# Pairs of score tiles, a new step order, and 8 KB rows for weight loads in a fused attention and soft-MoE kernel

## The chip, the cores and the metric

One core of a Trainium2 chip. TensorE (PE) does the matmuls, VectorE (DVE), ScalarE (ACT) and GpSimd (POOL) the rest; SyncE (SP) issues the DMAs from its queue, in order, and 16 DMA engines carry them. The metric is the device time of one execution in microseconds, as the median of several runs. The profiles come from the hardware profiler and hold one execution each.

## What is computed

```python
# 8 batches x 8 heads x 576 tokens x 64; attention only inside chunks of 64 tokens
scores = q_c @ k_c.T / 8
attn = softmax(scores)
x = (attn @ v_c)            # -> 4608 tokens x 512

logits = x @ phi            # 512 x 32: 8 experts x 4 slots
d = softmax(logits, over the 4608 tokens)
slot_input = d.T @ x        # 32 x 512
for e in range(8):
    slot_out[e] = relu(slot_input[e] @ w1[e]) @ w2[e]   # 512 x 1024, 1024 x 512
x = softmax(logits, over the 32 slots) @ slot_out

h = x @ w_in                # 4608 x 1024, 64-bit words on the host's side
u = h * softmax(h)
out = layernorm(u) * g_ln @ w_out
```

`moe2_w_in` and `moe2_w_out` reach the chip as 64-bit words, which the kernel itself turns into fp32.

## The kernel before, in words

The 4608 tokens are 36 tiles of 128. The program has three parts, and every engine's order is written out by hand, so an engine that waits holds up all that stands behind it on that engine.

**The loop over tiles** (L517, steps i = 0 to 33). A step works on several tiles at once: the scores `S` of tile i (`pe_S`, L251: per pair of heads two matmuls on column halves of PE), their maximum `mx`, the subtraction `sub` (L268) and `exp`; the transpose `PT` of tile i-1 and its copy `PTe`; the product with v, `x` (L295), of tile i-2 with its row sums `rz`, `rc` and the multiply `xm`; the transpose `xT` of tile i-3 and its copy `xTe`; every fourth step the logits `LT` and the running softmax over tokens (`lte`, `L`, `mT`, `z`, `sl`, `acc`). Beside it, from step 2, one of 32 chunks c of 64-bit words is converted on ACT, DVE and POOL (`sq`, `t`, `u`, `m`, `a`, `add`, `mul`). The order of the operations in a step is one of the four lines of `STEP` (L29), taken by i mod 4; an operation that a step doesn't have is skipped. The scores go to `sx`, one PSUM tile of two banks, bank i mod 2 (L249).

**Loads.** All are issued from SP, at the place of their name in the step: `qk` loads the keys and queries of tile i+4 into one of four buffers as two DMAs of 64 rows of 4 KB, on the even and on the odd partitions; `v` loads two tiles of v in every second step; `raw` (L185) loads the words of two chunks, 512 KB, into one of three buffers; `W` (L492) loads expert weights. These are 64 loads of 512 KB, m = 0 to 63, 4 KB on each of 128 partitions. `PACE` (L35) says how many are to be issued by each step. A load takes the next free place: first the 23 of the ring, and after the loop the buffers that the loop no longer needs, handed over by `own_c`, `own_q`, `own_v`, `own_p`, `own_t` and `own_x` (L787). `used_w` (L135) gives places back, two at a time, once the matmuls of two loads are issued; what is loaded there waits on SP for them. Before the loop `FIRST` (L44) issues the first loads.

**The expert tail** runs in the order of the list `ORDER` (L45): the last tiles, the slot inputs (`si`), then the experts' first layer `w1_...` (L932), the second layer `w2_...` (L968) and the last 16 loads' matmuls `wc48` to `wc63` (L982), which use the loads in the order of m. Between them stand transposes and copies for the next part. `x34` (L580) puts the product of tile 34 into `sx`.

**The loop over output tiles** (L1393 and around it) takes the second MLP for 36 tiles: 24 matmuls `o_ps` and two `h_ps` a tile, with the copies, the exponentials and two DMA transposes.

The lines of the step order before, and the weights' matmuls for one pair of loads:

```python
FIRST = "cs qk0 qk1 qk2 v0 raw0 qk3 g phi v2 raw2 raw4"
        for k in range(2):
            for j in range(4):
                nc.tensor.matmul(
                    h[32 * j:32 * j + 4, :], siT[:, 2 * kp + k, 4 * G + j, :], wt[m0 + 2 * k + j // 2][j % 2], ...
                )
            used_w(m0 + 2 * k, m0 + 2 * k + 1)
```

Of the kernel before, what the change touches and what calls it, by code (L numbers as in the profile page):

```python
# [9 lines left out]
F32 = mybir.dt.float32  # L10
# [3 lines left out]
U32 = mybir.dt.uint32  # L14
# [7 lines left out]
RING = 23  # L22
NRAW = 32
# [6 lines left out]
S a m t x xT u mT qk rz PT mx v xTe sub PTe W rc add mul raw exp xm mn d sq de  # L30
S a x u raw v m qk rz sl mx t W rc z xT sub xTe PT PTe add xm acc mul sq exp
m t S u a x qk rz xT mx W sub xTe PT rc acc v PTe add LT xm mul sq raw exp lte
t m a S x u raw L tm v mx xT add qk PT lall rz mul xTe sub rc PTe W sq xm exp
# [10 lines left out]
FIRST = "cs qk0 qk1 qk2 v0 raw0 qk3 g phi v2 raw2 raw4"  # L44
# [23 lines left out]
def soft_moe_kernel(ctx: ExitStack, tc, qkT, v1, w12, w64, phi, g_ln, cst, out):  # L68
# [49 lines left out]
    def w_tile(p):  # L118
        return lambda: [p.tile([128, 2, 512], F32, tag="w", name="w")]

    def load_w(n):
        while n > 0 and free and wloads:
            n -= 1
            m = wloads.pop(0)
            place[m] = free.pop(0)
            t = place[m]()
            if len(t) == 1:
                gated("w", nc.sync.dma_start(out=t[0], in_=w12[m]))
                wt[m] = [t[0][:, k, :] for k in range(2)]
            else:  # L130
                for k in range(2):
                    nc.sync.dma_start(out=t[k], in_=w12[m, :, k])
                wt[m] = t

    def used_w(*ms):  # L135
        for m in ms:
            if place[m] not in gone:
                free.append(place[m])
        load_w(len(free))

    gone = []
    free.extend([w_tile(ring)] * RING)
# [42 lines left out]
    def load_raw(c):  # L185
        if c < NRAW and c % 2 == 0:
            raw = cvp.tile([128, 2, 256, 2], U32, tag="raw", name="raw", bufs=3)
            raw_t[c], raw_t[c + 1] = raw[:, 0], raw[:, 1]
            gated("raw", nc.sync.dma_start(out=raw.rearrange("p k n t -> p (k n t)"), in_=w64[c // 2].bitcast(U32)))
# [45 lines left out]
    def cv_c(c):  # L235
# [4 lines left out]
        **{f"raw{i}": lambda i=i: load_raw(i) for i in range(6)},  # L240
# [8 lines left out]
    sx = ps1.tile([128, 2, 512], F32, name="s_ps")  # L249

    def pe_S(i):  # L251
        s = sx[:, i % 2, :]
# [218 lines left out]
    def step_ops(i):  # L471
# [9 lines left out]

        def rc():
# [9 lines left out]
        def W():  # L492
            load_w(pace[i + 1] - pace[i])
# [6 lines left out]
            S=(True, lambda: pe_S(i)), qk=(True, lambda: load_qk(i + 4)),  # L500
# [997 lines left out]
```

## Time and profile before

| | us |
|---|---|
| median of 3 runs | 403.44 (402.84 to 403.8) |
| the profiled execution | 402.77 |
| its span, first to last instruction | 401.0 |
| PE busy | 382.4 (95%) |
| DVE busy | 311.0 (78%) |
| ACT busy | 224.3 (56%) |
| POOL busy | 200.2 (50%) |
| granted TensorE clock, mean | 1.000 of full |

The busy time of PE counts matmuls whose ends are modelled, and they overlap: a PE that is 95% busy need not be at its peak. PEld is PE's weight load, which shows the pace of the matmuls better. The DMA share is the mean busy time of the 16 engines; it can be a little over 1, since packets of one engine overlap. All times in the profile are counted from the first instruction. A row of the timeline is one or several like instructions: its start, the time they took together, engine and line, operands and count, and in brackets how long the engine had been idle and for whom it waited.

### The profile page before, as it was taken

To read this page: it belongs to the slowest core of one execution; us is meant where nothing else is said; L and a number is where in the kernel's file an instruction comes from. 1 tells how busy PE (TensorE), PEld (TensorE's weight loads), DVE (VectorE), ACT (ScalarE), POOL (GpSimd) and SP (SyncE) were. 2 spreads that over 40 slices of the span, in tenths; PEclk is the share of its full clock that TensorE was granted. 3 is DMA by queue.
4 is the path that set the end of the run, shared out by engine and by line. 5 is a ranking of instruction groups with operands and counts; after the bars stand their busy time and mean duration, and the time that the engine had idled before them with its cause. 6 is when DMAs were issued, how large, how long until landed. Compare 5 with 4: busy or idle time off the path is not lost. (4 is left out here: it accounts for less than half of the span.)

```text
span 401.0 us, 10317 instructions
## 1 busy us (share of the span) xinstructions
PE 382.4 (95%) x3947; PEld 220.4 (55%) x3947; DVE 311.0 (78%) x777; ACT 224.3 (56%) x470; POOL 200.2 (50%) x201
## 2 busy tenths in 40 slices
PE   3799899999999999999999999999999999999997
PEld 2577777777787642354544444444444444444445
DVE  3788788989886449574989799999888888888840
ACT  1577877877785512332577765556554555455521
POOL 2577767777778246330123255555455544454430
PEclk9999999999999999999999999999999999999999
DMA  7999999999999999991156757777665666557671
GB/s 231 403 409 408 389 397 397 409 407 407 410 397 408 401 396 406 409 391 26 30 103 146 140 134 159 159 158 148 144 140 135 144 151 133 132 137 158 132 159 52
DMA packets 101153, 99.20 MB, mean 247 GB/s; under 512 B 78064, under 2 KB 78704, under 8 KB 101104
## 3 DMA queue, kind: packets, MB, share of 16 engines
q1 hardware_dynamic: 101104, 98.54, 77.1%
q8 instruction: 31, 0.51, 0.5%
q14 instruction: 18, 0.15, 0.1%
HBM read 70.60 MB, written 9.44 MB: 200 GB/s over the span
## 5 line engine op out<-in xcount | busy, mean ns | idle before, releaser
L1194 POOL TENSOR_SCALAR uh<-u,sc 128x1024 f16<-128x1024 f32 (+1 forms) x35 | 65.1, 1860 | 51.1 <-issue 38.3
L1393 PEld LDWEIGHTS <-uhT 128*128 128x128 f16 x560 | 52.1, 98 | 68.3 <-issue 8.8
L1393 PE MATMUL o_ps<-xb,uhT 128*128 128x512 f16 x280 | 66.7, 380 | 0.7 <-DMA uhT<-uh 0.7
L1393 PE MATMUL o_ps<-xb,ulT 128*128 128x512 f16 x280 | 66.3, 379 | 0.0
L1393 PE MATMUL o_ps<-wo,uhT 128*128 128x512 f16 x280 | 66.1, 379 | 0.0
L1322 ACT ACTIVATE e<-h_ps,nm 128x1024 f32<-128x1024 f32 x34 | 37.8, 1113 | 43.7 <-DVE nm L1316 43.7
L1210 ACT ACTIVATE e<-u,nmean 128x1024 f32<-128x1024 f32 x35 | 40.1, 1147 | 28.7 <-DVE nmean L1209 28.7
L256 PE MATMUL s_ps<-qk 128*64 128x128 f32 x576 | 41.1, 287 | 9.3 <-DMA qk<-in_qkT 6.5
L1360 POOL TENSOR_TENSOR a<-a,mhalf 128x1 f32<-128x1 f32 x36 | 21.8, 606 | 56.2 <-DVE a L1377 42.5
L1316 DVE TENSOR_REDUCE nm<-h_ps 128x1 f32<-128x1024 f32 x34 | 41.5, 1220 | 9.3 <-PE h_ps L1311 9.3
L1185 DVE SCALAR_TENSOR_TENSOR u<-h_ps,e 128x1024 f32<-128x1024 f32 x35 | 42.8, 1223 | 6.1 <-ACT e L1322 6.1
L1393 PEld LDWEIGHTS <-ulT 128*128 128x128 f16 x280 | 27.3, 98 | 33.1 <-issue 0.3
L1370 DVE SCALAR_TENSOR_TENSOR ul<-u,sc,uh 128x1024 f16<-128x1024 f32 x35 | 45.3, 1295 | 0.0
L256 PEld LDWEIGHTS s_ps<-qk 128*64 128x64 f32 x576 | 32.5, 141 | 16.2 <-issue 10.3
L398 ACT ACTIVATE xt_b<-xt_ps 128x512 f32<-128x512 f32 (+1 forms) x37 | 21.6, 586 | 17.8 <-PE xt_ps L416 16.9
L265 DVE TENSOR_REDUCE mx<-s_ps 128x8 f32<-128x512 f32 x36 | 24.6, 684 | 8.5 <-PE s_ps L256 8.0
L1411 ACT ACTIVATE ob<-o_ps,a 128x512 f32<-128x512 f32 x35 | 23.8, 679 | 9.3 <-PE o_ps L1393 8.0
L219 POOL TENSOR_SCALAR conv<-conv 128x256 f32<-128x256 f32 x16 | 17.6, 1099 | 21.8 <-ACT conv L206 21.8
L1311 PE MATMUL h_ps<-s,c4T 128*128 128x512 f32 x68 | 27.4, 485 | 0.0
L277 ACT ACTIVATE p<-p 128x512 f32<-128x512 f32 x35 | 21.7, 621 | 6.6 <-DVE p L271 6.6
L271 DVE TENSOR_TENSOR p<-s_ps,mx 128x512 f32<-128x512 f32 x35 | 24.1, 690 | 0.9
L229 POOL TENSOR_TENSOR conv<-conv 128x256 int32<-128x256 int32 x32 | 23.3, 729 | 2.6
(232 smaller groups left out, 633.5 us busy)
## 6 DMA issues: line engine op xcount, KB each, us to landing
w<-in_w SPq DMA_DIRECT2D x45, 512.0 KB, 8.0
qk<-in_qkT SPq DMA_DIRECT2D x72, 256.0 KB, 6.8
vall<-in_v SPq DMA_DIRECT2D x18, 520.0 KB, 6.7
out<-ob SPq DMA_DIRECT2D x35, 256.0 KB, 2.1
raw<-in_w SPq DMA_DIRECT2D x16, 512.0 KB, 6.4
qk<-in_w SPq DMA_DIRECT2D x4, 512.0 KB, 9.0
w_raw<-in_w SPq DMA_DIRECT2D x3, 512.0 KB, 9.0
vall<-in_w SPq DMA_DIRECT2D x3, 512.0 KB, 8.9
```

The costliest lines, as they stand in the source:

```text
L256: nc.tensor.matmul(s[ts(c, 64), ts(g, 128)], b[:, 1, ts(2 * g + c, 64)], b[:, 0:3:2, ts(2 * g + c, 64)], start=True, stop=True, tile_posit ...
L265: mark("mx", nc.vector.tensor_reduce(out=mx, in_=s, axis=AX.X, op=ALU.max))
L271: mark("sub", nc.vector.tensor_tensor(out=p, in0=s, in1=mx.unsqueeze(2).to_broadcast([128, 8, 64]), op=ALU.subtract,))
L1185: nc.vector.scalar_tensor_tensor(out=u, in0=d["h"], scalar=1.0, in1=e, op0=ALU.mult, op1=ALU.mult, accum_out=zz[:, 1:2])
L1194: nc.gpsimd.tensor_scalar(out=uh[:, 0:n], in0=u[:, 0:n], scalar1=d["sc"][:, 1:2], scalar2=1.0, op0=ALU.mult, op1=ALU.mult)
L1210: nc.scalar.activation(out=d["e"], in_=d["u"], func=AF.Square, bias=nmean, scale=1.0, accum_out=d["zz"][:, 2:3])
L1311: nc.tensor.matmul(h[:, ts(n, 512)], c4T[:, i, :], s4[n], start=True, stop=True)
L1316: nc.vector.tensor_reduce(out=nm, in_=st[i]["h"], axis=AX.X, op=ALU.max, negate=True)
L1322: nc.scalar.activation(out=d["e"], in_=d["h"], func=AF.Exp, bias=d["nm"], scale=1.0, accum_out=d["zz"][:, 0:1])
L1370: nc.vector.scalar_tensor_tensor(out=ul, in0=d["u"], scalar=d["sc"][:, 1:2], in1=d["uh"], op0=ALU.mult, op1=ALU.subtract)
L1393: nc.tensor.matmul(d["o"], lt(n % 8), w(n % 8), start=(n == 0), stop=(n == 23))
L1411: nc.scalar.activation(out=ob, in_=d["o"], func=AF.Copy, scale=d["a"][:, 7:8])
```

## The change

Six things are changed together.

- `S` of a step with even i computes the scores of tiles i and i+1; odd steps have none. The two banks are two tiles (`s_banks`) in a pool of their own, which is closed in `x34`, where `sx` is made.
- The four lines of `STEP` are new.
- `FIRST` ends with `phi qk3`; `v2` and `raw2` are issued behind the `qk` load of step 0, and `raw4` behind that of step 1 (`THEN`).
- Expert weights are stored in pairs, 8 KB a partition. The ring is 11 places of two loads (22 in place of 23). A pair is loaded by `halves`: one DMA of 64 rows of 8 KB for the even partitions, one for the odd. Where only a place of one load is free, a load goes there in rows of 4 KB as before. Some of the loop's buffers are handed over as places of two (`raw0`, `raw1`, `v0`, `xt`), and they can be used again.
- The 64-bit words are stored and loaded four chunks at a time, 1 MB, into one of two buffers, also by `halves`; the first eight chunks come as four loads of two chunks in rows of 4 KB as before.
- `W` counts by the places that are free, so that the ring is filled to `PACE`.

```diff
@@ -19,7 +19,7 @@
...
-RING = 23
+RING = 11
...
@@ -27,10 +27,10 @@
...
-S a m t x xT u mT qk rz PT mx v xTe sub PTe W rc add mul raw exp xm mn d sq de
-S a x u raw v m qk rz sl mx t W rc z xT sub xTe PT PTe add xm acc mul sq exp
-m t S u a x qk rz xT mx W sub xTe PT rc acc v PTe add LT xm mul sq raw exp lte
-t m a S x u raw L tm v mx xT add qk PT lall rz mul xTe sub rc PTe W sq xm exp
+S x t v m a rz xT u qk xTe PT mT PTe mx W sub add rc exp mul xm mn sq d raw de
+S mx xT qk x PT a u sub z m W raw add PTe rz sl exp t rc mul xm v acc xTe sq
+S m mx t x u W a acc xT rz PT xTe raw add LT mul sub rc PTe v sq exp lte qk xm
+x u S qk a m v t add rz mx sub xT L raw PT tm PTe rc xTe mul xm lall sq exp W
...
@@ -41,7 +41,8 @@
...
-FIRST = "cs qk0 qk1 qk2 v0 raw0 qk3 g phi v2 raw2 raw4"
+FIRST = "cs qk0 qk1 qk2 v0 raw0 g phi qk3"
+THEN = {0: 'v2 raw2', 1: 'raw4'}
...
@@ -115,31 +116,55 @@
...
-    def w_tile(p):
-        return lambda: [p.tile([128, 2, 512], F32, tag="w", name="w")]
+    def halves(out, in_):
+        for a in range(2):
+            nc.sync.dma_start(out=out[a:128:2], in_=in_[a:128:2])
+    def ring_place():
+        return ring.tile([128, 4, 512], F32, tag="w", name="w")
...
     def load_w(n):
...
-            n -= 1
-            m = wloads.pop(0)
-            place[m] = free.pop(0)
-            t = place[m]()
-            if len(t) == 1:
-                gated("w", nc.sync.dma_start(out=t[0], in_=w12[m]))
-                wt[m] = [t[0][:, k, :] for k in range(2)]
+            m = wloads[0]
+            wide = [f for f in free if f[0] == 2]
+            one = [f for f in free if f[0] == 1]
+            if m % 2 == 0 and wide and free[0][0] == 2:
+                if n < 2:
+                    return
+                f = wide[0]
+            elif one:
+                f = one[0]
...
-                for k in range(2):
-                    nc.sync.dma_start(out=t[k], in_=w12[m, :, k])
-                wt[m] = t
+                return
+            free.remove(f)
+            n -= f[0]
+            t = f[1]()
+            for k in range(f[0]):
+                place[wloads.pop(0)] = f
+            if f[0] == 2:
+                halves(t, w12[m // 2])
+                for k in range(4):
+                    wt.setdefault(m + k // 2, []).append(t[:, k, :])
+            else:
+                src = w12[m // 2, :, ts(m % 2, 2), :]
+                if len(t) == 1:
+                    nc.sync.dma_start(out=t[0], in_=src)
+                    wt[m] = [t[0][:, k, :] for k in range(2)]
+                else:
+                    for k in range(2):
+                        nc.sync.dma_start(out=t[k], in_=src[:, k])
+                    wt[m] = t
+    def places():
+        return sum(f[0] for f in free)
...
     def used_w(*ms):
-        for m in ms:
-            if place[m] not in gone:
-                free.append(place[m])
-        load_w(len(free))
-    gone = []
-    free.extend([w_tile(ring)] * RING)
+        f = place[ms[0]]
+        if f[0] == 2:
+            free.append(f)
+        load_w(places())
+    free.extend((2, ring_place) for _ in range(RING))
...
@@ -183,10 +208,16 @@
...
     def load_raw(c):
-        if c < NRAW and c % 2 == 0:
-            raw = cvp.tile([128, 2, 256, 2], U32, tag="raw", name="raw", bufs=3)
-            raw_t[c], raw_t[c + 1] = raw[:, 0], raw[:, 1]
-            gated("raw", nc.sync.dma_start(out=raw.rearrange("p k n t -> p (k n t)"), in_=w64[c // 2].bitcast(U32)))
+        if c < NRAW and c % 4 == 0:
+            raw = cvp.tile([128, 4, 256, 2], U32, tag="raw", name="raw", bufs=2)
+            for k in range(4):
+                raw_t[c + k] = raw[:, k]
+            raw_t["q", c // 4] = raw.rearrange("p k n t -> p (k n t)")
+            if c >= 8:
+                halves(raw_t["q", c // 4], w64[c // 4].bitcast(U32))
+        if c < 8 and c % 2 == 0:
+            b = slice(512 * (c % 4), 512 * (c % 4) + 1024)
+            nc.sync.dma_start(out=raw_t["q", c // 4][:, b], in_=w64[c // 4].bitcast(U32)[:, b])
...
@@ -246,10 +277,13 @@
...
-    sx = ps1.tile([128, 2, 512], F32, name="s_ps")
+    pss = ctx.enter_context(ExitStack())
+    ps_s = pool("ps_s", 1, pss, space=PSUM)
+    s_banks = [ps_s.tile([128, 512], F32, name="s_ps", tag=f"s{a}") for a in range(2)]
+    sx = None
...
     def pe_S(i):
-        s = sx[:, i % 2, :]
+        s = s_banks[i % 2]
...
@@ -479,6 +513,11 @@
...
+        def q():
+            load_qk(i + 4)
+            for o in THEN.get(i, "").split():
+                first_loads[o]()
         def rc():
...
@@ -490,14 +529,14 @@
...
         def W():
-            load_w(pace[i + 1] - pace[i])
+            load_w(pace[i + 1] - 22 + places())
...
         return dict(
...
-            S=(True, lambda: pe_S(i)), qk=(True, lambda: load_qk(i + 4)),
+            S=(i % 2 == 0, lambda: (pe_S(i), pe_S(i + 1))), qk=(True, q),
...
@@ -578,6 +617,9 @@
...
     def x34():
+        nonlocal sx
+        pss.close()
+        sx = pool("ps_sx", 1, pss, space=PSUM).tile([128, 2, 512], F32, name="s_ps")
...
@@ -761,8 +803,8 @@
...
     def raw_home():
-        raw = cvp.tile([128, 2, 256, 2], U32, tag="raw", name="w_raw", bufs=3)
-        return [raw.rearrange("p k n t -> p k (n t)").bitcast(F32)]
+        raw = cvp.tile([128, 4, 256, 2], U32, tag="raw", name="w_raw", bufs=2)
+        return raw.rearrange("p k n t -> p k (n t)").bitcast(F32)
...
     def p_pair():
...
@@ -772,12 +814,12 @@
...
     homes = dict(
-        raw0=raw_home, raw1=lambda: raw_home(), raw2=lambda: raw_home(),
+        raw0=(2, raw_home), raw1=(2, raw_home),
...
-        v=lambda: [va[:, 0:1024].rearrange("p (a b) -> p a b", a=2)],
-        **{f"v{i}": lambda i=i: [va[:, ts(i, 1024)].rearrange("p (a b) -> p a b", a=2)] for i in (1, 2)},
+        v0=(2, lambda: va[:, 0:2048].rearrange("p (a b) -> p a b", a=4)),
+        v2=lambda: [va[:, ts(2, 1024)].rearrange("p (a b) -> p a b", a=2)],
...
-        xt0=lambda: [XT[:, 0:2].rearrange("p t g n -> p t (g n)")], xt1=lambda: [XT[:, 2:4].rearrange("p t g n -> p t (g n)")],
+        xt=(2, lambda: XT.rearrange("p t g n -> p t (g n)")),
...
@@ -786,17 +828,15 @@
...
     def own(*names):
...
-            free.append(homes[k])
-            if k[0] not in "vp":
-                gone.append(homes[k])
-        load_w(len(free))
-    op("loadw")(lambda: load_w(len(free)))
-    op("own_c", "S34 x32 loadw")(lambda: own("qk0", "qk1", "qk2", "qkx", "raw0", "raw1", "raw2", "conv"))
+            free.append(homes[k] if isinstance(homes[k], tuple) else (1, homes[k]))
+        load_w(places())
+    op("loadw")(lambda: load_w(places()))
+    op("own_c", "S34 x32 loadw")(lambda: own("qk0", "qk1", "qk2", "qkx", "raw0", "raw1", "conv"))
...
-    op("own_v", "x34 x351 own_q")(lambda: own("v", "v1", "v2", "pt"))
+    op("own_v", "x34 x351 own_q")(lambda: own("v2", "v0", "pt"))
...
-    op("own_t", "own_p LT35")(lambda: own("xt0", "xt1"))
+    op("own_t", "own_p LT35")(lambda: own("xt"))
...
@@ -1475,10 +1516,10 @@
     arrays = {
...
-        "w12": np.stack(w12),
+        "w12": np.stack(w12).reshape(32, 2, 128, 2, 512).transpose(0, 2, 1, 3, 4).reshape(32, 128, 4, 512),
...
-            bits64(inputs["moe2_w_in"]).reshape(4, 128, 2, 512).transpose(0, 2, 1, 3).reshape(8, 128, 512),
-            bits64(inputs["moe2_w_out"]).reshape(8, 128, 512),
+            bits64(inputs["moe2_w_in"]).reshape(4, 128, 1024),
+            bits64(inputs["moe2_w_out"]).reshape(4, 2, 128, 512).transpose(0, 2, 1, 3).reshape(4, 128, 1024),
...
```

## Rows read from the trace of the kernel before

**Rows 1.** The page: span, and DMA share in 40 slices, in tenths

```profile
span 401.0 us, 10317 instructions
...
DMA  7999999999999999991156757777665666557671
```

**Rows 2.** The chain of waits that ended last: start us, us, what

```profile
206.86 5.35 PE o_ps L1393 x24
```

**Rows 3.** Windows: us, busy us of PE, PEld, DVE, ACT, POOL, clock, DMA, GB/s

```profile
20.00:120.00 100.00, 96.68 (x1932) 76.46 (x1927) 86.46 (x215) 76.80 (x202) 75.47 (x88) 1.00 1.02 403
145.00:183.50 38.50, 37.35 (x457) 15.63 (x460) 27.52 (x53) 9.51 (x17) 18.09 (x16) 1.00 0.99 376
```

**Rows 4.** Timeline of all engines, 172 to 206 us

```profile
171.88 0.33 SPq L128 DMA_DIRECT2D w<-in_w  x1
...
182.63 1.08 PE L987 MATMUL h_ps<-w,hTb 128*4 128x128 f32 x32
...
183.50 1.06 PE L1112 MATMUL sw_ps<-wi,soT 128*32 128x512 f32 x8
```

**Rows 5.** DMA issues, 171 to 173 us: count, KB each, us to landing

```profile
w<-in_w SPq DMA_DIRECT2D x1, 512.0 KB, 10.4
```

**Rows 6.** Waits of PEld, 126 to 184 us: us in total, times, longest

```profile
PEld h_ps L936 <- DMA w<-in_w: 1.0, 3, 0.3
```

**Rows 7.** DMA, 153 to 171 us: packets, MB, share of 16 engines

```profile
DMA packets 2022, 7.36 MB, mean 409 GB/s; under 512 B 226, under 2 KB 226, under 8 KB 2021
...
q1 hardware_dynamic: 2021, 7.34, 102.4%
```

**Rows 8.** DMA, 149.9 to 152.3 us

```profile
DMA packets 444, 0.95 MB, mean 395 GB/s; under 512 B 52, under 2 KB 52, under 8 KB 444
...
q1 hardware_dynamic: 444, 0.95, 104.8%
```

**Rows 9.** DMA, 52.5 to 53 us, then 43.5 to 44 us

```profile
q14 instruction: 1, 0.01, 3.9%
...
q14 instruction: 1, 0.01, 4.0%
```

**Rows 10.** DMA issues of the whole page: median us to landing last

```profile
qk<-in_qkT SPq DMA_DIRECT2D x72, 256.0 KB, 6.8
```

**Rows 11.** Timeline of PE, 123 to 126 us

```profile
123.37 1.97 PE L256 MATMUL s_ps<-qk 128*64 128x128 f32 x32
125.27 0.66 PE L416 MATMUL xt_ps<-cs,xb 128*128 128x128 f32 x4
```

**Rows 12.** Timeline of all engines, 71.9 to 76 us

```profile
72.01 1.09 PE L256 MATMUL s_ps<-qk 128*64 128x128 f32 x16
73.04 0.56 PEld L282 LDWEIGHTS x_ps<-vall,pt 64*64 64x64 f32 x32 [0.17 <-ACT p L277]
73.04 0.70 PE L282 MATMUL x_ps<-vall,pt 64*64 64x65 f32 x32
...
73.83 0.60 PE L416 MATMUL xt_ps<-cs,xb 128*128 128x128 f32 x4
...
74.20 0.17 ACT L304 ACTIVATE rz<-x_ps 128x8 f32<-128x8 f32 x1
...
74.86 1.24 PE L256 MATMUL s_ps<-qk 128*64 128x128 f32 x16
75.02 0.69 DVE L487 TENSOR_TENSOR xb<-x_ps,rz 128x512 f32<-128x512 f32 x1
```

**Rows 13.** Waits of PEld, 20 to 126 us

```profile
PEld s_ps L256 <- DVE p L271: 3.1, 11, 0.6
```

**Rows 14.** Timeline of PE, 0 to 34 us

```profile
19.39 1.09 PE L256 MATMUL s_ps<-qk 128*64 128x128 f32 x16 [1.01 <-DMA qk<-in_qkT]
```

**Rows 15.** Timeline of PE, 70 to 90.5 us

```profile
85.88 1.09 PE L256 MATMUL s_ps<-qk 128*64 128x128 f32 x16
```

**Rows 16.** Windows, one of 1 us

```profile
3.00:4.00 1.00, 0.00 (x0) 0.00 (x0) 0.04 (x1) 0.00 (x0) 0.00 (x0) 1.00 0.95 307
```

More of the change, by code (lines that the diff above doesn't have):

```diff
@@ L239, in soft_moe_kernel @@
         qk0=lambda: load_qk(0), qk1=lambda: load_qk(1), qk2=lambda: load_qk(2), qk3=lambda: load_qk(3), v0=lambda: load_v(0), v2=lambda: load_v(2),
-        **{f"raw{i}": lambda i=i: load_raw(i) for i in range(6)},
+        **{f"raw{i}": lambda i=i: load_raw(i) for i in range(6)}, v4=lambda: load_v(4), v6=lambda: load_v(6),
         cs=lambda: nc.sync.dma_start(out=cs, in_=cst), phi=lambda: nc.sync.dma_start(out=phi_sb, in_=phi),
@@ L872, in open_2 @@
         nonlocal e1, ps2, soT, cz, mx
+        pss.close()
         p1.close()
```

## The prediction

> **What bounds the kernel now.** I read the page first: a span of 401.0 us, in which the DMA engines are full for the first 18 of 40 slices, idle for two and half busy afterwards [rows 1]. Then the chain of waits: from 206.86 us to the end it is TensorE's (PE) `o_ps` and `h_ps` matmuls back to back, 5.35 us for a tile's 24 `o_ps`, with nothing to wait for [rows 2]. The diff touches no line that runs there, so the last 194 us have a fixed length, and the question is when they may begin.
>
> The windows split what lies before. In the loop over tiles (20 to 120 us) three resources are nearly full at once: DMA share 1.02 at 403 GB/s, PE busy 97 of 100 us, VectorE (DVE) 86 of 100. In the expert tail (145 to 183.5) PE is busy 37 of 38.5 us and the DMAs' share is still 0.99 [rows 3]. So two chains run side by side up to 183.5 us, where the last expert matmuls end: PE's order, and the stream of loads. The timeline shows how close they are: the last 512 KB of weights is issued at 171.88 and lands 10.4 us later, at 182.3; the matmuls that end the experts (m = 62 and 63) run from 182.63 to 183.50 [rows 4, 5]. PE's waits for weights before that are 1.0 us in all [rows 6]. **Both chains end within half a microsecond of each other**: a gain in one alone gives almost nothing, and the gain of the change is the smaller of its two gains.
>
> **The loads.** The change leaves the bytes and the number of DMAs as they are and replaces rows of 4 KB on 128 partitions by rows of 8 KB on 64. Which ones: the ring takes 22 weight loads (512 KB each) in the loop, and m = 42 to 63 again in the tail; in between I follow the list of free places through `own_c` to `own_x`: m = 26 to 29 (raw), 34, 35 (v0) and 38, 39 (XT) are wide, the other 12 stay single. That is 52 of 64 weight loads, and all but the first four of 16 conversion loads. So 64 DMAs of 64 rows: 4,096 wide rows in place of 8,192, 256 for each of the 16 engines.
>
> What a wide row costs no load shows, so I bound it. A 4 KB row: from 153 to 171 us, where only weights move, 1,795 packets of at least 512 B took 102.4% of 16 engines' 18 us, 164 ns each (the small ones taken as nothing); by the 409 GB/s that they moved it is 160 ns, since their times overlap a little [rows 7]. A 2 KB row: from 149.9 to 152.3, 392 such packets with 0.95 MB are by size 320 of 2 KB and 72 of 4 KB; 104.8% of 16 times 2.4 us, less 72 x 164 ns, leaves 89 ns. Two of them less one of 4 KB is 14 ns that comes once per row [rows 8]. An 8 KB packet exists, a fetch by queue 14 among the loads: 3.9% of 16 times 0.5 us is 312 ns, in another window 4.0%, 320 ns [rows 9]. Against 2 x 164 it saves 8 to 16 ns, against 2 x 160 up to 8 ns. 256 rows give 4.1 us at the most and 2.0 us by the better packet against the pace that loads really keep; the lower end is nothing, or a loss (first and third rival). I take 2.0 us, since the nearest row is an 8 KB packet itself. The last landing then moves from 182.3 to 180.3.
>
> The Trainium skill speaks against this part: "DMA: Bandwidth & Descriptors", section "Rules for kernel authors", says that two transfers to disjoint halves of the partitions gain nothing over one on 128 partitions, since they go one after the other through the same engines; by that the landing stays at 182.3, which is the first rival's sum. Its section "Why small descriptors are slow" gives a fixed 3 cycles a packet, which at the page's 850 MHz is an estimate of 0.9 us for 256 rows; the difference of the 2 KB and 4 KB rows here is larger.
>
> What the wide places give back: a pair of m can be used only when both its DMAs have landed. Before, m = 62 could run ahead of the last landing; now both groups follow it, and they take 0.87 us (182.63 to 183.50) [rows 4]. With 0.1 us to start: 180.3 + 0.1 + 0.87 = 181.3, **2.2 us before 183.5**. A reload also needs a whole pair of places, but `used_w` already freed two at a time. The ring holds 22 instead of 23, so one load moves out of the loop; a load lands about 7 us after its issue [rows 10], so the queue is never empty there, and a load's place in the stream costs nothing.
>
> **PE.** Scores of two tiles take 1.90 us from start to the next instruction (the kernel already does tiles 34 and 35 so, 123.37 to 125.27) [rows 11]; a single one takes 1.03 (72.01 to 73.04) [rows 12]. That saves 0.16 us a pair, 2.7 us over 17 pairs. The gap ahead of the scores falls away in odd steps and one ahead of `x` comes instead: nothing. Scores now wait 3.1 us in all, 11 times, for the subtraction of the tile before, though it reads the other bank (one tile spans both) [rows 13]; with a tile for each bank they wait for a subtraction a step older. Where the operation's kind changes PE's weight loads stop for about 0.17 us anyway [rows 12], so 3.1 - 11 x 0.17 = 1.2 us go. At the start, tile 4 waits 1.01 us for its qk load [rows 14]. `v2`, `raw2` and `raw4` are moved on SP behind qk3, qk4 and (raw4) qk5, 1.57 MB or 3.9 us of the stream at 403 GB/s, so these tiles come sooner and the first conversions later; ScalarE and GpSimd are 75 to 77% busy in the loop and catch up [rows 3]. I count 0 to 1.5 us, and take 0.5.
>
> New waits: qk of an odd tile is issued in its old step but used a step earlier, so three steps ahead: 10.4 us, as four steps take 13.87 (72.01 to 85.88) [rows 12, 15]. A load lands after 6.8 us [rows 10]; a 1 MB pair or raw group in front, where there was 0.5 MB, makes it 1.3 us later each, and that is still in time. On SP each raw group waits for the conversion that frees its buffer, half as often as before, with `W`, `v` and qk queued behind it; as long as that wait is under the queue's 6.8 us no engine sees it. What the new order of `xT`, `PT` and `x` does I bound by nothing and by the second rival. PE thus gains 2.7 + 1.2 + 0.5 = 4.4 us, between -3.3 and 5.4. **The smaller gain is the loads' 2.2 us**; PE then waits for weights inside the tail, which is what is late next.
>
> **The sum.** The experts end at 181.3 in place of 183.5, all behind it is unchanged: span 398.8. The profiled execution took 402.77 us, 1.8 of it outside the span; the median of the three runs is 403.44, 0.7 above it, and 2.2 less is 401.2. About 0.2% (0.8 us) is what a measurement of this kernel can tell from no change.
>
> **The rivals.** First, wide rows bring nothing: 320 ns for an 8 KB packet is twice 160. The landing stays, 182.3 + 0.97 = 183.3, so 403.2, whatever PE gains. For it speaks the second packet of [rows 9]; against it the 2 KB rows. 18%.
>
> Second, slower by the new order. `xT` of a tile now stands first in the second step of four, with one pair of transposes (73.83 to 74.86, 1.03 us) between it and the tile's `x`. `x` ends at 73.74 (73.04 + 0.70), its row sums start at 74.20, the multiply that `xT` needs ends at 75.71: 1.97 us [rows 12]. If DVE is no faster there, PE waits 0.9 us every four steps, 7.7 us in 8.5 rounds; less the 4.4 it is 3.3 us later: 406.7. It decides from 0.5 us a round on. Against it: DVE has 14% free, and in the rows it was at another tile's subtraction first. 10%.
>
> Third, loads of 64 rows are slow by themselves. From 3 to 4 us only qk loads (64 rows of 4 KB) move, at 307 GB/s with share 0.95: 0.95 x 16 us for 75 rows of 4 KB, 203 ns a row, not 164 [rows 16]. If the tail's stream of 22 such loads (11.5 MB, 28.2 us at 409 GB/s) is 20% longer, it ends 5.6 us later, 409. It decides as soon as a wide row takes over 330 ns. Against it: qk loads are a third of the loop's bytes, and the loop still moves 403 GB/s against 409 [rows 3, 7], so that is how a stream starts. 6%.
>
> **The numbers.** The forecast's own case has 66%, from 399.3 (4.1 us by the dearest reading of the rows) to 402.6. The range goes on to 404.2, which takes in the first rival and small stalls of the second's kind. Faster by over 0.2%: 66% and a piece of the first rival, 70%; within it 17%; slower 13%.
>
> **What would show it.** Packets of 8 KB at 305 to 316 ns and 415 to 420 GB/s in the tail; the last weights landing near 180; score pairs of 1.9 us that wait for no subtraction; the expert tail starting 2 to 5 us earlier, with waits for weights inside it. The forecast is wrong if wide rows take 320 ns or more, if `xT` or the scores wait in each round, or if the last landing moves and 183.5 does not.

## The result, and the profile after

The changed kernel took 407.45 us (median of 4 runs, 405.42 to 410.79) beside 403.62 us for the kernel before (402.84 to 404.19): ratio 1.0105, 95% interval 1.0061 to 1.0149. It is slower by 1%; the forecast was 401.2, range 399.3 to 404.2. The profiled execution took 409.39 us; its span is 407.6 us, 6.6 more than before [rows 1]. Medians here and below are over all runs of a kernel; ratios leave out a run more than 1.5% above its kernel's fastest, one each of two kernels below.

From the page after: span, granted clock and DMA share in 40 slices, the packets of the load queue, and the shares of the chain that ended last.

```profile
span 407.6 us, 10330 instructions
...
PEclk9899999999999989999999999999999999999999
DMA  6999999999999999990066656777656665587681
...
DMA packets 97057, 99.20 MB, mean 243 GB/s; under 512 B 78064, under 2 KB 78704, under 8 KB 92912
...
PE 82%; DVE 6%; ACT 4%; DMA 3%; issue 2%; POOL 2%; SPq 1%; DVEq 0%; ACTq 0%
```

The windows of the loop and of the expert tail (columns as in [rows 3]; the tail begins 6 us later), and the last expert matmuls:

```profile
20.00:120.00 100.00, 94.27 (x1875) 75.53 (x1873) 85.77 (x210) 74.01 (x197) 74.82 (x86) 1.00 1.01 399
151.00:189.50 38.50, 37.35 (x458) 15.63 (x460) 27.51 (x53) 9.54 (x17) 18.07 (x16) 1.00 0.86 345
```

```profile
188.62 1.08 PE L1028 MATMUL h_ps<-w,hTb 128*4 128x128 f32 x32
189.50 1.06 PE L1153 MATMUL sw_ps<-wi,soT 128*32 128x512 f32 x8
```

The experts end at 189.50 in place of 183.50 [rows 4], and TensorE (PE) is the bound: in the tail the DMAs' share is 0.86, not 0.99, and in the loop PE is busy 94.3 us of 100, not 96.7 [rows 3]. The two traces, set side by side at three marks, say where the time went (timeline; tile 6 before, then tiles 6 and 34 after):

```profile
25.27 1.09 PE L256 MATMUL s_ps<-qk 128*64 128x128 f32 x16
```

```profile
27.30 1.97 PE L290 MATMUL s_ps<-qk 128*64 128x128 f32 x32
127.28 1.97 PE L290 MATMUL s_ps<-qk 128*64 128x128 f32 x32
```

Tile 6's scores start 2.03 us later. Tile 34's start at 127.28 in place of 123.37 [rows 11], another 1.88. The first expert matmul starts at 150.97 in place of 144.97, another 2.09. From there to the end of the experts nothing changes. The 0.6 behind them is one longer wait: `o_ps` waits 1.3 us for a DMA transpose, 0.7 before.

In the tail the loads did what was forecast of a single row. From 171 to 178 us, where only 8 KB rows move (DMA view; before: 409 GB/s [rows 7]):

```profile
DMA packets 453, 2.94 MB, mean 420 GB/s; under 512 B 94, under 2 KB 94, under 8 KB 94
...
q1 hardware_dynamic: 453, 2.94, 101.6%
```

So PE is late before the tail begins. Three things show in its timeline. At the **start** it idles before the scores of tile 3, with `x` of tile 0 behind them in its order, and then the granted clock is 0.50 for 3.2 us (timeline, and windows with columns as above; the wait in the second row is put down to a subtraction, but the first group of experiments shows that it was for the load `qk3`):

```profile
10.53 1.39 PE L290 MATMUL s_ps<-qk 128*64 128x128 f32 x16
14.83 1.98 PE L290 MATMUL s_ps<-qk 128*64 128x128 f32 x16 [2.90 <-DVE p L305]
16.74 1.15 PE L316 MATMUL x_ps<-vall,pt 64*64 64x65 f32 x32
```

```profile
11.90:14.80 2.90, 0.03 (x2) 0.00 (x0) 2.01 (x4) 1.08 (x3) 0.72 (x1) 0.97 1.04 405
14.80:18.00 3.20, 3.17 (x49) 2.75 (x50) 0.00 (x0) 0.05 (x1) 1.83 (x3) 0.50 0.98 370
```

The same 16 matmuls take 1.98 us at the low level (1.2 GHz) and 1.09 at 2.4 GHz [rows 12]. In the **loop** `xT` waits for VectorE (DVE), and PE also stops in the middle of a group of `x` matmuls, for nothing that the profile shows:

```profile
51.53 0.46 PE L316 MATMUL x_ps<-vall,pt 64*64 64x65 f32 x15 [0.48 <-issue]
81.11 0.63 PE L450 MATMUL xt_ps<-cs,xb 128*128 128x128 f32 x4 [0.39 <-DVE xb L526]
104.97 0.35 PE L316 MATMUL x_ps<-vall,pt 64*64 64x65 f32 x8 [1.52 <-issue]
132.36 0.60 PE L359 MATMUL lt_ps<-xt_b,phi_sb 128*32 128x128 f32 x10 [0.68 <-issue]
```

**Behind the loop** the clock is 0.50 once more:

```profile
144.30:147.70 3.40, 3.40 (x24) 1.95 (x28) 0.60 (x4) 1.18 (x5) 0.00 (x0) 0.50 1.00 405
```

3.4 us of work at half speed is 1.7 us lost. With two smaller ones (0.35 at 38.06, 0.21 at 91.11) the stops come to 3.2 us; the kernel before has one, of 0.26. 2.0 (start) + 3.0 (stops beyond that one) + 1.7 (clock) is 6.7, against 6.0 lost up to the end of the experts. The 0.7 between them lies in the loop, where 2.6 us of stops cost 1.88. The runs seem to differ by such events: of these four, two with a mean clock of 1.0 took 405.4 and 405.5, two with falls 409.4 and 410.8.

### The profile page after: what moved, and what is told of

Same layout as the page of the kernel before. It is cut to its first block, busy times and chain, and to the rows that moved or that the text cites. A ratio compares the mean times of both kernels' runs of the same rounds, so it can differ in the third digit from the quotient of the medians.

```text
span 407.6 us, 10330 instructions
## 1 busy us (share of the span) xinstructions
PE 385.2 (95%) x3947; PEld 223.4 (55%) x3947; DVE 312.3 (77%) x777; ACT 223.8 (55%) x470; POOL 201.4 (49%) x201
## 4 chain that ended last, share of the span: by engine, by line
PE 82%; DVE 6%; ACT 4%; DMA 3%; issue 2%; POOL 2%; SPq 1%; DVEq 0%; ACTq 0%
PE o_ps L1434 43%; PE s_ps L290 6%; PE x_ps L316 4%; PE h_ps L1352 4%; PE xt_ps L450 4%; PE h_ps L977 3%; PE pt_ps L441 3%; PE h_ps L1028 2%; DMA raw<-in_w 2%; PE h_ps L1014 2%; PE lt_ps L359 2%; PE sl_ps L501 1%; DVE xb L526 1%; PE o_ps L1444 1%; PE c_ps L960 1%
## 5 line engine op out<-in xcount | busy, mean ns | idle before, releaser
L290 PE MATMUL s_ps<-qk 128*64 128x128 f32 x576 | 38.8, 290 | 8.6 <-DMA qk<-in_qkT 5.3
L290 PEld LDWEIGHTS s_ps<-qk 128*64 128x64 f32 x576 | 33.6, 145 | 16.9 <-issue 15.4
L432 ACT ACTIVATE pt<-pt_ps 128x512 f32<-128x512 f32 x35 | 20.9, 597 | 12.7 <-PE pt_ps L441 12.7
L316 PE MATMUL x_ps<-vall,pt 64*64 64x65 f32 x1088 | 25.0, 227 | 3.0 <-issue 2.0
L450 PE MATMUL xt_ps<-cs,xb 128*128 128x128 f32 x140 | 22.8, 284 | 3.8 <-DVE xb L526 2.1
```

The source lines that it names most:

```text
L290: nc.tensor.matmul(s[ts(c, 64), ts(g, 128)], b[:, 1, ts(2 * g + c, 64)], b[:, 0:3:2, ts(2 * g + c, 64)], start=True, stop=True, tile_posit ...
L316: nc.tensor.matmul(x[ts(c, 64), a, ts(g, 65)], pt[ts(a, 64), ts(c, 64)], vall[ts(a, 64), i % 6, ts(2 * g + c, 65)], start=True, stop=True, ...
L432: A=lambda o, i: nc.scalar.activation(out=o, in_=i, func=AF.Copy),
L450: nc.tensor.transpose(t[:, g, :], x_t[i][:, ts(g, 128)], ident)
```

## The experiments

Theories at the outset: A, the new first loads and order of steps make PE late; B, inside the loop the order gives back what pairs save; C, the wide loads delay PE. "Tile 6 to 34" is the time between those tiles' first scores, 98.10 us before and 99.98 after. A "stop" is an idle time of PE that the profile puts down to issue.

**1. The parts, and the start.** First the loads alone (old STEP, FIRST and single scores).

> The new loads (8 KB rows, 11 pair places, raw groups of four, wide homes) with the old order of steps, single scores and the old order of the first loads. Theory A (the new order of the first loads and steps makes TensorE late; the loads are innocent): TensorE's order is that of before, so 402.5 to 403.6, with weights landing about 2 us earlier than in the kernel before and a granted clock of 1.0. Theory C (the wide loads themselves delay TensorE, by the unexplained stops inside groups of x matmuls at 51.5, 105.0 and 132.4 us of the changed kernel): those stops come back, 2 to 3 us, so 405 to 407.

404.87 us, ratio 1.0045 (1.0021 to 1.0068). In between: the loads are not innocent. The profile has stops of 1.18 us at 50.0, 0.53 at 135.5 and 0.69 at 182.8. They sum to the 2.4 us by which its span is longer, but that is not where the time went: tile 6 starts 1.33 us late, behind a wait of 1.22 for tile 5's `qk`; tile 6 to 34 takes 97.57, less than before in spite of its stop; and 1.2 us (the third stop among them) come between the first and the last expert matmul.

Then the order alone (new STEP, FIRST, THEN, pairs; old loads):

> The new order of steps and of the first loads, scores of two tiles, a tile of PSUM for each bank, with the old loads of 4 KB rows. Theory A: TensorE is as late as in the changed kernel, 3 to 6 us at the first expert matmul (before: 144.97 us), score pairs of tile 4 on about 2 us later than single ones were, a clock of 0.5 near 15 us: 405 to 409. Theory C: without wide rows the order gives its gain on TensorE but the loads bind as before: 402.5 to 403.6.

406.50, ratio 1.0067 (1.0043 to 1.0091), as theory A; but the start was hardly late in this profile (tile 6 at 25.43, PE waiting 1.25 for `qk3`), and tile 6 to 34 took 99.4. The two parts' ratios add up to that of the whole.

Then qk3 earlier:

```diff
-FIRST = "cs qk0 qk1 qk2 v0 raw0 g phi qk3"
+FIRST = "cs qk0 qk1 qk2 qk3 v0 raw0 g phi"
```

> The changed kernel with one edit: qk3 stands before v0 and raw0 in the first loads. Theory A1 (the second score pair waits for qk3's landing at about 14.7 us, with x(0) behind it, and the clock falls in that pause): S(3) starts about 2 us earlier, the clock does not fall at 15 us, every later score is 1.5 to 2.5 us earlier, and the time is 403.5 to 406. Theory A2 (the second pair is late because the first conversion waits for raw0 and holds up the subtraction of tile 2 on VectorE): the start stays as late, since raw0 lands later still; 407 to 409.

Tile 3's scores follow tile 2's at once, as A1 says, so that wait was for `qk3`. But the pause only moves: the next `x` waits for VectorE, which A1 did not expect, and the clock falls there, at 18.2 us:

```profile
16.39 0.70 PE L316 MATMUL x_ps<-vall,pt 64*64 64x65 f32 x32 [2.12 <-DVE xb L526]
```

Tile 4 starts at 19.48 in place of 20.96, and tile 6 at 26.29 in place of 27.30: half of the start's 2.0 us. It took 409.90, ratio 1.0126 (1.0068 to 1.0184). In the one execution profiled, the longest of the four (412.61), six stops, five of them 0.76 to 1.74 us, come to 6.3 us, and tile 34 starts at 130.8. A1 is right about that wait and far from the whole.

The changed kernel again:

> The changed kernel again, beside the three others, for its spread and its clock on the same chip. All theories: 405.4 to 410, with the fall of the granted clock to 0.5 near 15 us in each profile; if the runs near 405.5 have no such fall, the clock's part of the loss is the difference, 3 to 4 us.

408.17, ratio 1.0107 (1.0068 to 1.0146). The first loads again let PE wait 1.8 us for qk3; here matmuls ran at half speed until 23 us although the granted clock shows no fall, and tile 6 started at 28.95. Stops of 0.66 and 0.24. So with the new first loads the start cost 0.2 (order alone), 2.0 and 3.7 us: it varies.

**2. Rows or bookkeeping? Which of x and xT first?** The loads-only kernel with column halves (4 KB rows on 128 partitions) in the same places:

```diff
-        for a in range(2):
-            nc.sync.dma_start(out=out[a:128:2], in_=in_[a:128:2])
+        q = out.shape[1] // 2
+        for k in range(2):
+            nc.sync.dma_start(out=out[:, ts(k, q)], in_=in_[:, ts(k, q)])
```

> The loads-only kernel with its bookkeeping (pair places, raw groups of four, the order of the loads), but each pair is loaded as two halves of the columns, 4 KB rows on 128 partitions, instead of 8 KB rows on 64. Theory C1 (rows of 8 KB make the queue run low and stop in the loop): the loads-only kernel's loss goes, 403.0 to 403.8; lost time of the load stream from 20 to 145 us back from 4 to about 2 us. Theory C2 (the loss comes from raw groups of four in two buffers, and pair places, whatever the rows): as the loads-only kernel, 404.5 to 405.5.

405.79, ratio 1.0059 (1.0036 to 1.0082): C1 falls, the size of the rows is not it. The loads-only kernel with 8 KB rows from m = 22 on:

> The loads-only kernel with 8 KB rows only from weight m = 22 on, that is behind the loop over tiles; in the loop 4 KB rows as in the run beside it. Theory C1: no loss in the loop, and the tail's stream ends about 1.5 us earlier; TensorE's order is that of before, so 402.6 to 403.6. Theory C2: 404.5 to 405.5. If wide rows cost something in the tail too (the loads-only kernel took 1.2 us longer there): 404 to 405.

404.92, ratio 1.0045 (1.0020 to 1.0071): not C1, but within the range of C2 and of the third case, which it does not separate. The order-only kernel with `x` ahead of `xT`:

```diff
-S mx xT qk x PT a u sub z m W raw add PTe rz sl exp t rc mul xm v acc xTe sq
+S mx x xT qk PT a u sub z m W raw add PTe rz sl exp t rc mul xm v acc xTe sq
```

> The order-only kernel with x ahead of xT in the second step of four. Theory B (what score pairs save, about 0.4 us in four steps, is given back where xT waits for VectorE's product one x earlier, 0.3 to 0.6 us): the wait for xb goes, a round of four steps takes 13.4 to 13.6 us in place of 14.0, tiles near 120 us are reached 2 to 3 us earlier than in the order-only kernel; 403.0 to 405, since the loads bind next. Theory B2 (the loop's pace is set by the load stream, not by TensorE's waits): xT no longer waits, but scores wait for qk instead, and the time stays at 405.2 to 407.

407.07, ratio 1.0082 (1.0062 to 1.0103). Neither B nor B2: `xT` waits no more, but `x` now stands behind the transposes whose eviction it needs, and waits 0.64 us in each round (timeline; one of seven):

```profile
80.35 0.27 PE L427 MATMUL mT_ps<-cs,ltb 128*128 128x128 f32 x1
81.26 0.70 PE L286 MATMUL x_ps<-vall,pt 64*64 64x65 f32 x32 [0.64 <-ACT pt L402]
```

All three edits in the changed kernel (x first, qk3 early, wide rows from m = 22):

> The changed kernel with three edits: x ahead of xT in the second step, qk3 ahead of v0 in the first loads, 8 KB rows only from weight m = 22 on. If theories B and C1 both hold, TensorE reaches the experts 1 to 3 us before the kernel before does and the last weights land 1.5 us earlier: 401.5 to 403.5. If the loop is paced by its loads (B2) or the raw groups (C2): 404.5 to 407.

408.71, ratio 1.0126 (1.0095 to 1.0157): no repair, with stops of 0.32, 1.06, 0.70 and 0.38.

**3. Each term by itself.** Pairs on the old order (S in even steps only, two score tiles):

> The kernel before with score pairs alone: in even steps the scores of two tiles into two separate PSUM tiles, none in odd steps; the order of all other steps and all loads as before. Theory B3 (what a pair saves is lost again, because in a step without scores nothing stands between a transpose and the x that waits for its eviction, nor between x and the next transposes): a round of four steps takes 14.3 us or more in place of 13.87, with waits of x for pt or of xT for xb of 0.4 us or more in each odd step: 406 to 412. The prediction's sum (pairs gain 2.7 us and the separate tiles 1.2 us on TensorE, loads bind next): rounds of 13.4 us, 402.5 to 403.6.

411.48, ratio 1.0187 (1.0143 to 1.0231), a round of 14.4 us where nothing stops. From 26 to 126 us (waits of PE):

```profile
PE x_ps L285 <- ACT pt L401: 4.6, 6, 0.8
PE sl_ps L470 <- ACT d L451: 2.0, 6, 0.4
PE x_ps L285 <- issue: 1.3, 1, 1.3
```

B3 holds: a step without scores has nothing to put between a transpose and its `x`. Separate score tiles alone:

```diff
-    sx = ps1.tile([128, 2, 512], F32, name="s_ps")
...
+    s_banks = [ps_s.tile([128, 512], F32, name="s_ps", tag=f"s{a}") for a in range(2)]
...
```

> The kernel before with one PSUM tile for each score bank in place of one over both, nothing else. The prediction's term: the scores' waits for a subtraction (3.1 us in 11 places) fall to a tenth or so, and tile 34 is reached 1.2 us earlier; the time is then set by the loads, 402.9 to 403.6. Rival: the subtraction was only the last of several things that scores wait for; they wait for qk or the transposes instead, and tile 34 comes at 123.4 as before, 403.4.

406.84, ratio 1.0076 (1.0049 to 1.0102), which neither expects: the wait at 32.7 us goes, but tile 34 comes 3.1 us later, with stops of 0.90 and 1.01 before it and 0.36 behind. The stops leave more than 1 us of that unexplained. Wide weights alone, and wide raw groups alone:

> Wide weights alone: weight loads as 8 KB rows in pair places, raw loads in pairs of 4 KB rows and three buffers, order of steps as before. Theory C3 (loads given to the queue 1 MB at a time leave it short in between; a load that starts under about 2.2 us behind its issue has slow packets): 8 to 12 such loads from 20 to 145 us, in place of 7 before and 16 with both parts, the stream 0.2 to 0.3 MB behind, 403.8 to 404.6. If the weights' pairs are innocent: 402.5 to 403.5.

> Wide conversion loads alone: raw groups of four, 8 KB rows in two buffers, a ring of 22 single weights, order of steps as before. Theory C3: 8 to 12 loads that start under 2.2 us behind their issue, the stream 0.2 to 0.3 MB behind, 403.8 to 404.6. If the raw groups are the whole cause (theory C2): 404.5 to 405.5.

404.77, ratio 1.0022 (0.9992 to 1.0051), and 404.22, ratio 1.0012 (0.9984 to 1.0039): inconclusive, a little slower at most. C3's count fails: 16 and 17 loads began within 2.2 us of the end of their issue, not 8 to 12. But the first shows what one stop costs (timeline and windows):

```profile
51.04 0.88 PE L440 MATMUL xt_ps<-cs,xb 128*128 128x128 f32 x4 [1.94 <-issue]
```

```profile
49.10:51.00 1.90, 0.00 (x1) 0.07 (x1) 1.61 (x4) 0.29 (x2) 1.74 (x3) 1.00 1.01 404
51.00:53.60 2.60, 2.56 (x15) 2.23 (x16) 1.24 (x6) 1.11 (x3) 0.24 (x1) 0.54 1.03 412
```

PE stands for 1.9 us, then works at a clock of 0.54: between tiles 12 and 14 that execution loses 2.85 us against the kernel before, of the 3.5 by which its span is longer.

**4. What the stops are.** Every change with the full stream of loads, in whatever place, brought stops: 0.35 to 6.3 us of them from 26 to 146 us, where the kernel before has 0.26 (one execution each). Counted in weight loads (PEld), those of the changed kernel fall here (windows from 0 to each stop, PEld count in brackets):

```profile
0.00:51.40 51.40, 40.06 (x718) 32.49 (x719) 34.84 (x79) 29.35 (x73) 28.80 (x41) 0.97 0.94 354
0.00:104.80 104.80, 90.33 (x1724) 72.36 (x1724) 81.86 (x196) 68.96 (x178) 69.09 (x87) 0.98 0.98 377
0.00:132.30 132.30, 116.18 (x2226) 93.09 (x2227) 105.11 (x254) 87.63 (x227) 90.46 (x109) 0.99 0.98 381
```

1724 - 719 = 1005 is 8 x 125.6, and 2227 - 1724 = 503 is 4 x 125.75. 126 weight loads and as many matmuls, with PE's semaphore instructions, are some 256 instructions; the page's instruction queue (q8) moves 16 KB packets, 64 bytes for each of 256. In the 20 profiles of this study, those below among them, PE has 52 stops of 0.2 us and more from 26 to 146 us. All 52 fall on this grid (within 5 weight loads), none beside it, and PE goes on 1.23 to 1.56 us after the end of such a packet. At the other 288 block bounds that the 20 loops cross, PE passes some 1.2 us or more after the packet's end, half of the time over 2.0: never sooner. For the stop before 104.97 (DMA windows 102.7 to 103.75 and 103.75 to 105; the packet ends at 103.69):

```profile
q1 hardware_dynamic: 58, 0.39, 94.1%
q8 instruction: 1, 0.02, 5.7%
...
q1 hardware_dynamic: 95, 0.48, 91.8%
```

So theory F: **PE waits for its own instructions**, whose fetches share the DMA engines with the loads. Two kernels shift the grid, two take the weights out of the loop (PACE all 0; 64 weight loads behind it, so they end late and only the loop is read).

> The kernel before without weight loads inside the loop over tiles (all 64 come behind it), so that a quarter of the loop's load stream is gone. It will end late for that, and only the loop is read: tile 6 to tile 34, 98.1 us in the kernel before. Theory F (TensorE runs close behind the fetches of its own instructions, which land later while the queue of loads is busy): fetches land under 4 us behind the block before them, no stop of TensorE over 0.5 us, and the loop takes 96 to 98 us. If TensorE's order alone sets the loop: 97.8 to 98.2 us.

> The changed kernel without weight loads inside the loop, read beside the run of the kernel before without them: tile 6 to tile 34, 99.98 us in the changed kernel. Theory F: fetch stops (3 us in its first profile) go, and what is left is the order's own time, 97 to 98 us, some tenths from the other run, since the pairs' 0.4 us and the shorter gaps in four steps are given back by the waits of xT. If the order itself costs the 2 us: 99.5 us or more, with the waits as before. The prediction's sum: 94 to 95 us.

Waits of PE from 26 to 126 us and the scores of tiles 6 and 34, in the kernel before without weights in the loop, then in the changed one:

```profile
PE sl_ps L464 <- ACT d L445: 1.0, 4, 0.2
PE s_ps L253 <- DVE p L268: 0.9, 3, 0.3
PE lt_ps L322 <- ACT zacc L377: 0.3, 1, 0.3
...
26.19 1.09 PE L253 MATMUL s_ps<-qk 128*64 128x128 f32 x16 [0.33 <-DVE p L268]
123.83 1.97 PE L253 MATMUL s_ps<-qk 128*64 128x128 f32 x32
```

```profile
PE xt_ps L447 <- DVE xb L523: 2.9, 6, 0.6
PE L_ps L387 <- ACT ltb L372: 0.5, 1, 0.5
PE xt_ps L447 <- issue: 0.3, 1, 0.3
...
25.15 1.97 PE L287 MATMUL s_ps<-qk 128*64 128x128 f32 x32
122.98 1.97 PE L287 MATMUL s_ps<-qk 128*64 128x128 f32 x32
```

No stop in the first, one of 0.30 in the second. Tile 6 to 34 takes 97.64 and 97.83 us. As far as one execution of each can tell, that is the order's own worth: **the new order neither gains nor loses**; its 2 us in the loop were stops (2.6 in that stretch). By the packets' records the fetches end 3.3 and 3.9 us after the weight load that begins the block before (mean of 17 blocks), against 4.5 before and 5.0 after.

The shift:

```diff
...
+    for _ in range(30):
+        nc.tensor.matmul(sx[0:8, 0, 0:8], zero, zero, start=True, stop=True)
```

> The kernel before with 30 small matmuls of zeros on TensorE while it waits for its first load; nothing else. They shift the bounds of its 16 KB instruction blocks by 30 weight loads of some 125. Theory F, strong form (the kernel before is quick because its block bounds fall where there is time): stops of 0.5 us and more appear at other places of the loop, and the time is 404.5 to 407. Weak form (only lateness of a fetch counts): 403 to 404, with few stops, as before. If the stops have nothing to do with instruction blocks: no change, 403.4, and any stop falls at the places it had.

405.43, ratio 1.0055 (1.0032 to 1.0078), from 30 matmuls that PE does while it would wait. The strong form holds for the time; the one execution profiled (span 402.6) has only a stop of 0.48 us before 104.64, under the 0.5 that was named, and a small one before 131.62, both at places where the kernel before has none (windows from 0):

```profile
0.00:104.60 104.60, 95.27 (x1847) 75.61 (x1848) 83.66 (x204) 72.19 (x185) 70.89 (x89) 1.00 0.99 387
0.00:131.50 131.50, 120.99 (x2349) 95.78 (x2349) 104.97 (x258) 90.27 (x234) 92.54 (x112) 1.00 1.00 388
```

> The changed kernel with the same 30 small matmuls at the start. Theory F: stops of TensorE move with the blocks, to places 30 weight loads earlier in the program than 719, 1724 or 2227 plus multiples of 125.65 counted with the 30; their sum may be larger or smaller, 404 to 410. If stops belong to the program's own places (a wait that the profile doesn't name): they stay with the same matmuls, and the time is that of the changed kernel.

408.12, ratio 1.0120 (1.0078 to 1.0162), with five stops:

```profile
0.00:48.70 48.70, 37.58 (x720) 30.72 (x720) 32.63 (x76) 26.93 (x67) 27.36 (x40) 0.96 0.94 357
0.00:63.30 63.30, 50.70 (x971) 41.18 (x971) 44.48 (x104) 37.37 (x94) 36.99 (x51) 0.97 0.95 363
0.00:109.60 109.60, 94.98 (x1850) 76.72 (x1851) 85.24 (x204) 71.70 (x185) 71.58 (x89) 0.98 0.98 376
0.00:117.80 117.80, 101.91 (x1975) 81.97 (x1976) 91.65 (x222) 76.97 (x199) 77.23 (x95) 0.99 0.98 379
```

With the 30 counted the stops stand at 720, 971, 1851, 1976 (and 2354), within two of 719 plus 0, 2, 9, 10 and 13 times 125.65: they moved with the blocks, 30 weight loads towards the front of the program. That PE waits for fetches is shown.

**5. Dose, and the score tiles.** Half the weights in the loop, and the separate score tiles without any:

> The changed kernel with half the weight loads in the loop over tiles (12 of 22 by its end). It ends late for that, and only the loop is read, between the changed kernel (99.98 us from tile 6 to tile 34, fetches landing 5.1 us behind the block before them) and the run without weights in the loop (97.82 us, 3.9 us). Theory F: fetches land 4.0 to 4.9 us behind, stops of TensorE sum to 0 to 1.5 us, the loop takes 97.8 to 99.3 us. If the stops don't depend on the load stream: 100 us.

> The kernel before with one PSUM tile for each score bank, without weight loads in the loop; read beside the kernel before without weights in the loop (97.64 us from tile 6 to tile 34). Theory F: with the fetch stops gone, the separate tiles show their own worth: 96.4 to 97.6 us, the scores' waits for the subtraction (0.3 us each, 3 to 4 left there) gone. If the separate tiles themselves cost the 0.8% that they cost with the full load stream: 99 us or more.

Theory F misses both times, and both times the rival's number came. The first: fetches at 4.6 us, as expected, but a stop of 1.31 (and one of 0.42), and 99.92 us, where the rival said 100. The second: 99.66 us, where the rival said 99 or more, with a stop of 0.76 before 102.78 and fetches at 4.1 us; the other waits behind its 2 us are small and I can't add them up, so separate tiles may cost something of their own. Fetches end sooner with less load on the queue; that stops go with the load is not shown, since one execution of each kernel says little and these two stopped with less load, again on the grid.

## Why the prediction was wrong

**The step that failed** is "PE thus gains 2.7 + 1.2 + 0.5 = 4.4 us, between -3.3 and 5.4", and with it "The smaller gain is the loads' 2.2 us". PE gained nothing: its experts end 6.0 us later, and the loop's order by itself, without weight loads, takes as long as before (97.83 and 97.64 us).

- Pairs, 2.7: the size was right (in the order-only kernel two pairs take 3.80 us of a round up to the next instruction; four single scores took 4.13), but it doesn't stay. I bounded the new order by nothing and by the second rival, and put that at 10%. The rival's wait, `xT` for VectorE, came in six of seven rounds, at a smaller price: 0.3 to 0.6 us, not 0.9. Without weight loads in the loop nothing of the saving is left.
- Separate tiles, 1.2: the wait at 32.7 us goes, and no time comes of it; alone they cost 0.8%.
- The start, "0 to 1.5 us, and take 0.5": wrong in sign. I looked at qk of tile 4 and took qk3 to come sooner. It stands behind `v0` and `raw0` as before, and now behind `g` and `phi` too: its first DMA is issued at 7.51 us, 6.42 before. PE's new order has tile 3's scores ahead of `x(0)`, so their wait became PE's, and the clock fell in that pause: 2.0 us in this profile. With qk3 ahead of `v0` that wait goes; another, of `x` for VectorE, takes its place, and one of the 2.0 us stays. Its cause I did not follow up.
- What no term held: PE's instructions are loads too. The trace of before had the signs, a stop of 0.26 at 134.47 and the q8 packets, and the prediction passes over both. In the changed kernel the stops (3.0 us) and the fall of the clock behind the loop (1.7) are more than the other 4 us. A model with PE's durations and named waits could not give this. Why the changed kernel's fetches are late more often than those of the kernel before stays open.

**Point by point on the rest.** 8 KB rows: right in the tail, where 420 GB/s was the upper end of what I said would show it. In the loop they brought nothing: from 20 to 120 us an 8 KB packet took 330 ns on average (1,919 of them), two 4 KB packets of the kernel before 327. The Trainium skill's rule against two transfers on halves of the partitions ("DMA: Bandwidth & Descriptors", section "Rules for kernel authors") doesn't hold in this tail, where the halves bring rows of twice the size (420 GB/s against 409). But the last weights did not land at 180.3: some 30 packets of 8 KB begin after 182 us, and the last ends at 184.2; before, the last weight packet ended at 181.8. "The queue is never empty there, and a load's place in the stream costs nothing" failed. The changed kernel's stream is 0.8 MB behind at 50 us and 0.9 at 180. Of the 0.8, the loads-only kernel has 0.4 and the order-only kernel 0.1. One part is that SP issues in larger lumps with longer pauses; how much, and how much comes of PE giving buffers back late, is not shown. SyncE's timeline:

```profile
35.88 2.71 SPq L201 DMA_DIRECT2D qk<-in_qkT  x4
41.15 1.11 SPq L121 DMA_DIRECT2D raw<-in_w  x2
```

No load is issued for 2.56 us there, while the raw group waits for the conversion that frees its buffer. From 42 to 44 us the queue (DMA view) moves 258 GB/s:

```profile
DMA packets 105, 0.52 MB, mean 258 GB/s; under 512 B 21, under 2 KB 21, under 8 KB 65
```

The lag might have cost the end something had PE been on time: in the run with column halves the last matmuls did wait for a weight (0.58 us, until 184.63). As it was, PE ended 6 us later and the loads had room. Both chains moved the wrong way, and the rule "the smaller gain decides" was applied to two gains, neither of which came.

No version here beats the kernel before. Its loop is within 0.5 us of its time without weights (98.10 and 97.64, one execution each).

## What to carry to other kernels

A PE stream of small matmuls consumes instructions by the block, and with the DMA engines full their fetch can become PE's next wait. Before you shorten the gaps of such a loop, look for idle times put down to issue and ask how far ahead of its use each block lands; a change that costs no time of its own can lose by where the block bounds fall, as the 30 small matmuls did (0.55%). And a saved instruction is only a gain if its cover is not needed: in a loop where each op waits for an eviction, the op you merge was what hid it.

## What the runs showed of the hardware

- **Instruction fetch.** After a stop PE goes on 1.23 to 1.56 us after the end of a 16 KB fetch, and at none of 340 block bounds sooner than some 1.2; fetches end 3.3 to some 5.4 us (means of a run's 17 blocks) after PE entered the block before, in blocks that last some 6.6 us. The Trainium skill says of such a crossing that it is mostly hidden ("Runtime: NRT & Kernel Launch", section "Instruction fetch mechanics", which also gives the 16 KB and 256 instructions): the grid agrees; in this loop it is not hidden, at up to 1.94 us. Why a fetch ends late in one block and not in another I could not settle; with the bytes then queued it goes only weakly (a correlation of 0.34 over the 340 blocks).
- **A load that starts soon after its issue is slow.** From 20 to 145 us, loads whose first packet moves within 1.5 us of the end of their issue have 8 KB packets of some 400 ns (23 loads in the runs with all weights in the loop), those later than 3 us 315 to 322 ns (means of a run). 7 of 128 loads before, and 14 of 126 after, started within 2.2 us.
- **A pause can cost twice.** The granted clock went to 0.50 for 3.4 us at a stop of 1.94 us (wide weights alone) and at five waits of 2.1 to 3.2 us near the start (2.90 in the changed kernel); at one wait of 2.19 us (half the weights) the record shows no fall. The fall at 144.3 followed no such pause: PE was busy 3.20 of the 3.30 us before it. Its cause stays open.
